# A fused attention and MLP kernel: batch 2 transposed by the DMA crossbar, and an order of steps written out as a list

## The chip, the cores and the metric

The kernel runs on one core of a Trainium2 chip. The metric is the device time in microseconds of one execution. Engines are named as the profile names them: PE is TensorE (matmuls), with PEld its weight loads, DVE is VectorE, ACT is ScalarE, POOL is GpSimd, and SP is SyncE, which here only issues DMAs.

## The reference

There are 8 batches of 8 heads, 576 rows each, head size 64, and 32 "packed" queries p for each head. Attention is done twice: p attends to k and v, and then q attends to that packed result as both keys and values. Its output (4608 rows of 512) goes through an MLP with a hidden width of 2048 and a squared relu.

```python
def sm_attn(qq, kk, vv):
    s = scale * np.matmul(qq, kk.transpose(0, 1, 3, 2))
    ...
    a = a / (np.sum(a, axis=-1, keepdims=True) + 1e-09)
    return np.matmul(a, vv)
p_packed = sm_attn(p, k, v)
out = sm_attn(q, p_packed, p_packed)
...
r = np.maximum(x @ w_in, 0.0)
return (s * (r * r) + b) @ w_out
```

## The kernel before, in words

All inputs are float32 in memory. The loads go through POOL's DMA queue, which turns them into bfloat16 on the way. Each of k, q and v of a batch is one tile of 96 x 3072 from a pool of five buffers (the tag "raw"), which reordered copies of q and v share.

A batch goes through these steps. Each is a small function whose instructions are issued in the order in which the functions are called:

- `prep_p` transposes p on TensorE into `pbd`. `twice_p` first doubles p in its own tile with a VectorE copy.
- `prep_k(b, half)` transposes half of the keys with 12 TensorE transposes and one VectorE copy; `prep_q(b, half)` does the same for half of the queries with 24 transposes, a ScalarE copy and a VectorE copy. For later batches `dma_k` and `dma_q` do these transposes with the DMA crossbar from SP's queue instead; `dma_q` needs a reordered copy of q, made by `order_q` with two VectorE copies. `order_v` reorders v in the same way for a denser form of the matmuls in `packed`. Which form `packed` takes is set by the constant `N_PE_T`: batches below it are transposed on TensorE.
- `first_scores(b, qd)`: scores of p against k for half of the heads, and their exp on ScalarE. `packed(b, qd)`: weights times v, and the sums of the weights; with the second half VectorE makes `ppc` and the reciprocals `rd` and `rs`.
- `second_scores(b)`: q against the packed result, and the exp. `weights(b, qd)`: column sums by a matmul, logarithm and exp of their negative on ScalarE, and a VectorE product, which gives `aT`.
- `packed_w` (two quarters of w_in at a time) or `packed_w1` (one quarter): the packed result times w_in, scaled into `pw` by ScalarE and VectorE. The attention output itself is never formed: `mlp_in(b, m)` multiplies `pw` with `aT` for one of 16 blocks of the hidden width, ScalarE takes the relu into `rlu`, VectorE squares it into `gT`.
- `Out.step(n)`: n of the 16 matmuls of `gT` with `w_out` for one group of 128 output rows. With the last, VectorE applies s and the bias row `biasrep` into `ysb`, and SP stores it. The bias row itself is 16 matmuls (`bias_part`).

PSUM has three double banks for all steps but the last (tile `hps`), and two single banks for the outputs (tile `yps`). A step that needs a double bank waits until an earlier one has been read out.

The order is pinned for each engine: TensorE, VectorE, ScalarE, POOL and SP each work through their instructions as the code calls them. Up to batch 2's scores the calls are written out one below the other, with `idle(n)` in between: n dummy matmuls on a tile of zeros, 42 in all. Batches 0 and 1 share one MLP stretch. From batch 2 on, a loop over the 16 blocks m of batch b's MLP places the attention steps of batch b + 1 at fixed blocks, and fills up with output matmuls of the batch before:

```python
        for m in range(NFF):
            mlp_in(b, m)
            for f in steps.get(m, []):
                f()
            fill(per)
```

Of the kernel before, what the change touches and what calls it, by code (L numbers as in the profile page):

```python
# [8 lines left out]
BF16 = mybir.dt.bfloat16  # L9
AF = mybir.ActivationFunctionType  # L10
ALU = mybir.AluOpType


@with_exitstack
def kernel(
# [25 lines left out]
    P = 128  # L41
# [11 lines left out]
    HS = S // 2  # L53
    NT = S // P
    TAIL = S - NT * P
    N_PE_T = 3

    constp = ctx.enter_context(tc.tile_pool(name="constp", bufs=1))
    wpool = ctx.enter_context(tc.tile_pool(name="wpool", bufs=1))
# [36 lines left out]
    def load(store, src, b, tag, h0=0, h1=H):  # L96
        if h0 == 0:
            store[b] = raw(tag).rearrange("r (h x) -> r h x", h=H)
        pool.dma_start(
            out=store[b][:, h0:h1, :],  # L100
            in_=src[b, h0:h1].rearrange("h (r c) d -> r h (c d)", c=NC),
        )

    w_in_sb = wpool.tile([P, NKC, DFF], BF16, name="w_in_sb")
    w_out_sb = wpool.tile([P, NFF, NB], BF16, name="w_out_sb")
    gT = wpool.tile([P, NFF, 3 * S], BF16, name="gT")
# [2 lines left out]
    def load_p(b0, b1):  # L109
        pool.dma_start(  # L110
            out=pn[:, b0:b1, :, 0, :],
            in_=p[b0:b1].rearrange("b (q g) j d -> (g j) b q d", g=4),
        )

    def load_w_in(ch):
        w = moe_w_in[:, ch * NB:(ch + 1) * NB].rearrange("(x k d) f -> x d k f", x=2, d=D)
        for h2 in range(2):
            pool.dma_start(out=w_in_sb[D * h2:D * h2 + D, :, ch * NB:(ch + 1) * NB], in_=w[h2])

    def load_w_out(m0, m1):  # L120
# [7 lines left out]
    vec.memset(identb[:], 0.0)  # L128
    zeros = constp.tile([P, NB], BF16, name="zeros")
    vec.memset(zeros[:], 0.0)  # L130
    load(kn, k, 0, "kn", 0, 4)
    load_p(0, 2)
    load(kn, k, 0, "kn", 4, 8)
    pool.affine_select(
        out=identb[:], in_=identb[:], compare_op=ALU.not_equal, fill=1.0, base=0,
        pattern=[[-1, P]], channel_multiplier=1,
    )
    load(qn, q, 0, "qn")
    load(vn, v, 0, "vn")
    svec = constp.tile([P, 1], F32, name="svec")  # L140
    sp.dma_start(out=svec[:], in_=moe_s[0:1].unsqueeze(0).to_broadcast([P, 1]))
    bvec = constp.tile([P, 1], F32, name="bvec")
    sp.dma_start(out=bvec[:], in_=moe_b[0:1].unsqueeze(0).to_broadcast([P, 1]))
    nc.scalar.preload_act_table_set("natural_log_exp_and_others")
    load(kn, k, 1, "kn")
    load(qn, q, 1, "qn")
    load_w_in(0)
    load(vn, v, 1, "vn")
    load_w_out(0, 4)
    for ch in range(1, NCH):  # L150
        load_w_in(ch)
        load_w_out(4 * ch, 4 * ch + 4)

    KW = H * HS + 32
    kT = [constp.tile([P, KW], BF16, name=f"kT{i}") for i in range(2)]
    qT = [constp.tile([P, NC, HP, R], BF16, name=f"qT{i}") for i in range(2)]
# [16 lines left out]
    def idle(n):  # L173

        t = big()
        for x in range(n):
            mm(t[:, 0, :], zeros[:, 0:P], zeros[:], start=True, stop=True)

    load_p(2, B)


    aT, pw, vr, qr, e1, e2, rd, rs = {}, {}, {}, {}, {}, {}, {}, {}
# [234 lines left out]
    def slot(b):  # L417
        return 1 if b % 2 else (b % 4)
# [5 lines left out]
    def mlp_in(b, m, on_act=True):  # L424
        hps = big()
        for qd in range(NQ):
            for hf in range(2):
                mm(
                    hps[:, hf, 0:HS],
                    pw[b][:, qd, m * P:(m + 1) * P],  # L430
                    aT[b][:, qd, hf * HS:(hf + 1) * HS],
                    start=(qd == 0),
                    stop=(qd == NQ - 1),
                )
        rlu = ysp.tile([P, 2, HS], BF16, tag="rlu", name="rlu")
        if on_act:
            act.activation(out=rlu[:], in_=hps[:, :, 0:HS], func=AF.Relu)
        else:
            vec.tensor_scalar_max(out=rlu[:], in0=hps[:, :, 0:HS], scalar1=0.0)
        g0 = slot(b) * S  # L440
        (vec if on_act else pool).tensor_tensor(
            out=gT[:, m, g0:g0 + S].rearrange("p (a s) -> p a s", a=2),
            in0=rlu[:], in1=rlu[:], op=ALU.mult,
        )

    def bias_part(cps, m):
        mm(cps, onesb[:], w_out_sb[:, m, :], start=(m == 0), stop=(m == NFF - 1))
        if m == NFF - 1:
            vec.tensor_scalar_mul(out=biasrep[:], in0=cps, scalar1=bvec[:])

    def store(ysb, i0, b, col, n):

# [9 lines left out]
    class Out:  # L462


        def __init__(self, col, parts):
            self.col, self.parts, self.m = col, parts, 0

        def step(self, n):

            if self.m == 0:  # L470
                self.yps = psy.tile([P, NB], F32, tag="y", name="yps")
            m1 = min(self.m + n, NFF)
            for m in range(self.m, m1):
                mm(
                    self.yps[:],
                    gT[:, m, self.col:self.col + P],
                    w_out_sb[:, m, :],
                    start=(m == 0),
                    stop=(m == NFF - 1),
                )  # L480
            took = m1 - self.m
            self.m = m1
            if m1 == NFF:
                ysb = ysp.tile([P, NB], F32, tag="ysb", name="ysb")
                vec.scalar_tensor_tensor(
                    out=ysb[:], in0=self.yps[:], scalar=svec[:], in1=biasrep[:],
                    op0=ALU.mult, op1=ALU.add,
                )
                i0 = 0
                for b, col, n in self.parts:  # L490
                    store(ysb, i0, b, col, n)
                    i0 += n
            return took
# [22 lines left out]
        load(qn, q, b, "qn")  # L516
        load(vn, v, b, "vn")

    def m1(b, *ms):
        for m in ms:  # L520
            mlp_in(b, m)

    idle(11)
    twice_p(0, 2)
    prep_k(0, 0)
    prep_p(0)
    idle(7)
    prep_k(0, 1)
    first_scores(0, 0)
    idle(3)  # L530
    first_scores(0, 1)
    prep_p(1)
    idle(3)
    prep_q(0, 0)
    prep_q(0, 1)
    idle(6)
    packed(0, 0)
    packed(0, 1)
    idle(5)
    second_scores(0)  # L540
    prep_k(1, 0)
    prep_k(1, 1)
    weights(0, 0)
    first_scores(1, 0)
    weights(0, 1)
    first_scores(1, 1)
    loads(2)
    idle(3)
    packed_w1(0, 0)
    prep_q(1, 0)  # L550
    prep_q(1, 1)
    m1(0, 0, 1)
    idle(2)
    packed(1, 0)
    packed(1, 1)
    m1(0, 2, 3)
    second_scores(1)
    packed_w1(1, 0)
    idle(2)
    todo = outs(0)  # L560
    t0, t1 = todo[0], todo[1]
    todo = todo[2:]

    def fill(n):
        run_outs(todo, n)

    weights(1, 0)
    t0.step(4)
    weights(1, 1)
    t1.step(4)  # L570
    packed_w1(0, 1)
    m1(1, 0)
    packed_w1(1, 1)
    m1(1, 1, 2, 3)
    for c in range(1, NCH):
        for j in range(4):
            m1(0, 4 * c + j)
            if c > 1 or j > 1:
                (t0 if j % 2 else t1).step(2)
            m1(1, 4 * c + j)  # L580
            if c + 1 < NCH and j > 1:
                packed_w1(j - 2, c + 1)
    twice_p(2, B)
    bps = big()
    for m in range(NFF // 2):
        bias_part(bps[:, 0, :], m)
    prep_p(2)
    prep_k(2, 0)
    for m in range(NFF // 2, NFF):
        bias_part(bps[:, 0, :], m)  # L590
    prep_k(2, 1)
    t0.step(4)
    first_scores(2, 0)
    t1.step(4)
    first_scores(2, 1)
    fill(4)
    loads(3)
    prep_q(2, 0)
    fill(2)
    prep_q(2, 1)  # L600
    fill(4)
    packed(2, 0)
    fill(4)
    packed(2, 1)
    fill(6)
    second_scores(2)
    packed_w(2, 0)
    fill(6)
    weights(2, 0)
    fill(4)  # L610
    weights(2, 1)
    fill(4)
    packed_w(2, 1)
    dma_k(3)
    todo += outs(1)
    fill(10)

    for b in range(2, B):
        a = b + 1
        c = a + 1  # L620
        steps = {}

        def at(m, *fs):
            steps.setdefault(m, []).extend(fs)

        d = 3 if b == 2 else 0
        if b == 2:
            at(1, lambda: (order_q(3), dma_q(3)))
            at(2, lambda: (prep_p(3), order_v(3)))
        if a < B:  # L630
            at(0 + d, lambda: first_scores(a, 0))
            at(1 + d, lambda: first_scores(a, 1))
            at(3 + d, lambda: packed(a, 0))
            at(4 + d, lambda: packed(a, 1))
            at(6 + d, lambda: second_scores(a))
            at(8 + d, lambda: packed_w(a, 0))
            at(9 + d, lambda: weights(a, 0))
            at(10 + d, lambda: weights(a, 1))
            at(12 + d, lambda: packed_w(a, 1))
        if c < B:  # L640
            at(1 + d, lambda: loads(c))
            at(8 + d, lambda: dma_k(c))
            at(10 + d, lambda: (order_q(c), dma_q(c)))
            at(12 + d, lambda: order_v(c))
            at(14, lambda: prep_p(c))
        if b > 2:
            todo = outs(b - 1)
        per = len(todo)
        for m in range(NFF):
            mlp_in(b, m)  # L650
            for f in steps.get(m, []):
                f()
            fill(per)
        fill(NFF * (NT + 1))
    todo = outs(B - 1)
    while todo:
        fill(NFF)
# [1 line left out]
_INS = ['q', 'k', 'v', 'p', 'moe_w_in', 'moe_w_out', 'moe_s', 'moe_b']  # L659
_OUTS = [((4608, 512), 'float32')]  # L660
# [25 lines left out]
```

## Time and profile before

| | |
|---|---|
| median of 7 runs | 269.53 us (268.67 to 271.43) |
| profiled execution | 268.99 us, its span 267.2 us |
| TensorE busy | 249.4 us (93%), 2346 matmuls |
| ScalarE, VectorE busy | 144.2 us (54%), 142.9 us (53%) |
| matmuls into yps | 576, 143.7 us busy |
| matmuls pw x aT | 512, 82.1 us busy |
| dummy matmuls on zeros | 42, 13.7 us busy |
| relu on ScalarE | 128, 650 ns each |
| DMA moved | 34.32 MB, mean 128 GB/s |
| transposes by DMA | 5 of keys (median 5.0 us to landing), 5 of queries (10.4 us) |

Busy time counts an instruction from its start to its end. Matmuls overlap each other, so their busy times add up to more than the time from one start to the next, and a TensorE that is 93% busy still has gaps that the timeline shows better. A bracket at the end of a timeline row gives the idle time of the engine ahead of the row, and what ended it. "PEclk" is the clock that TensorE was granted, as a share of full speed. Time before the first matmul on data, at 7.54 us, is the wait for the first load. All bytes and rates of loads in this document are counted as bfloat16, as they arrive.

### The profile page before, as it was taken

Reading aid. Unit: us, or ns where it says so; the run is one execution under the profiler, and the core shown is the slowest. Engines: PE = TensorE matmul, PEld = TensorE weight load, DVE = VectorE, ACT = ScalarE, POOL = GpSimd, SP = SyncE. Lnnn points to the kernel's source line nnn. Section 1 sums busy time; section 2 is a strip of 40 time slices with the busy share of each in tenths; the row PEclk is TensorE's granted clock in tenths of the full one; section 3 lists DMA queues with packets and bytes.
Section 4 is the critical chain, followed back from the end, with each engine's and each line's share of the span. In section 5 each row is a group of like instructions: output and inputs, shape, how many; then the busy total and the mean of one; then the engine's idle time right before and its main releaser. Section 6 shows DMA issues by size and latency. Waiting matters only on the chain.

```text
span 267.2 us, 5645 instructions
## 1 busy us (share of the span) xinstructions
PE 249.4 (93%) x2346; PEld 139.2 (52%) x2346; DVE 142.9 (53%) x295; ACT 144.2 (54%) x219; POOL 29.4 (11%) x44
## 2 busy tenths in 40 slices
PE   6698889999999999799999999999999999999993
PEld 2364635555535564465556555665565555555441
DVE  2224657676337645765793459456944574444221
ACT  1047689882455537756855575548653773443000
POOL 8243342001000300101030012000000000000000
PEclk9799999999999999999999999999999999999999
DMA  3999999990914999599999969994731113111332
GB/s 39 196 205 204 206 206 196 204 194 4 162 49 94 157 219 177 105 173 198 168 114 154 210 128 161 117 225 92 131 88 42 39 39 82 40 39 42 79 79 79
DMA packets 54634, 34.32 MB, mean 128 GB/s; under 512 B 27472, under 2 KB 50000, under 8 KB 54608
## 3 DMA queue, kind: packets, MB, share of 16 engines
q0 software_dynamic: 25200, 18.61, 48.2%
q1 hardware_dynamic: 29408, 15.34, 26.8%
q8 instruction: 18, 0.29, 0.4%
q14 instruction: 8, 0.07, 0.1%
HBM read 37.23 MB, written 9.44 MB: 175 GB/s over the span
## 4 chain that ended last, share of the span: by engine, by line
PE 71%; DMA 11%; ACT 8%; DVE 6%; issue 2%; POOL 0%; DVEq 0%; ACTq 0%; POOLq 0%
PE yps L71 39%; PE hps L71 30%; DMA qT<-qr 6%; DMA pn<-in_p_dram 3%; PE hps L74 2%; ACT rlu L82 2%; DMA kT<-kn 2%; DVE pw L82 2%; ACT rcd L82 2%; ACT pw L82 2%; ACT e L82 2%; ACT ld L82 1%; DVE qr L82 1%; DVE gT L82 1%; DVE ysb L82 1%
## 5 line engine op out<-in xcount | busy, mean ns | idle before, releaser
L71 PE MATMUL yps<-w_out_sb,gT 128*128 128x512 bf16 x576 | 143.7, 379 | 0.2 <-DVE gT L82 0.2
L82 ACT ACTIVATE rlu<-hps 128x576 bf16<-128x576 f32 x128 | 81.7, 650 | 70.4 <-PE hps L71 63.5
L82 DVE TENSOR_TENSOR gT<-rlu 128x576 bf16<-128x576 bf16 x128 | 58.2, 456 | 67.0 <-ACT rlu L82 65.6
L71 PE MATMUL hps<-aT,pw 128*128 128x288 bf16 x512 | 82.1, 286 | 4.1 <-DVE pbd L82 1.5
L71 PEld LDWEIGHTS <-gT 128*128 128x128 bf16 x576 | 52.9, 98 | 50.3 <-issue 5.7
L71 PEld LDWEIGHTS <-pw 128*128 128x128 bf16 x512 | 49.1, 98 | 38.5 <-issue 5.5
L82 DVE SCALAR_TENSOR_TENSOR ysb<-yps,svec,biasrep 128x512 f32<-128x512 f32 x36 | 26.9, 746 | 14.0 <-PE yps L71 13.8
L82 DVE TENSOR_SCALAR pw<-hps,rd 128x1024 bf16<-128x1024 f32 (+1 forms) x20 | 21.3, 1066 | 4.6 <-ACT pw L82 2.0
L82 ACT ACTIVATE e<-hps 96x768 bf16<-96x768 f32 x16 | 12.8, 799 | 17.7 <-PE hps L71 17.7
L82 ACT ACTIVATE pw<-hps,rd 128x1024 bf16<-128x1024 f32 (+1 forms) x20 | 18.8, 939 | 0.8 <-PE hps L71 0.7
L82 DVE TENSOR_TENSOR aT<-e,rcd 128x576 bf16<-128x576 bf16 x16 | 12.1, 758 | 11.5 <-ACT rcd L82 11.4
L71 PE MATMUL hps<-zeros 128*128 128x512 bf16 x42 | 13.7, 467 | 2.5 <-DVE zeros L82 1.3
L82 POOL DMA_DIRECT2D kn<-in_k_dram x9 | 6.9, 770 | 77.9 <-DMA kT<-kn 52.6
L82 ACT ACTIVATE e<-hps,rs 128x576 bf16<-128x576 f32 x16 | 10.9, 738 | 8.0 <-PE hps L71 8.0
L71 PE MATMUL hps<-w_in_sb,ppc 64*32 64x512 bf16 x256 | 11.5, 382 | 1.1 <-ACT e L82 0.7
L82 ACT ACTIVATE rcd<-ld 128x576 f32<-128x576 f32 x16 | 10.9, 683 | 0.5
L82 ACT ACTIVATE ld<-hps 128x576 f32<-128x576 f32 x16 | 10.3, 643 | 1.0 <-PE hps L71 1.0
L82 POOL DMA_DIRECT2D vn<-in_v_dram x8 | 6.2, 774 | 42.2 <-PE hps L74 28.0
L71 PE MATMUL hps<-pbd,kT 128*128 128x64 bf16 x192 | 8.7, 193 | 1.5 <-DVE kT L82 0.9
L71 PEld LDWEIGHTS <-kT 128*128 128x128 bf16 x192 | 7.9, 98 | 3.4 <-DVE kT L82 1.3
L71 PEld LDWEIGHTS <-ppc 64*32 64x32 bf16 x384 | 4.2, 89 | 9.7 <-issue 8.6
L71 PEld LDWEIGHTS <-zeros 128*128 128x128 bf16 x42 | 4.5, 117 | 7.9 <-issue 5.4
(45 smaller groups left out, 114.9 us busy)
## 6 DMA issues: line engine op xcount, KB each, us to landing
qn<-in_q_dram POOLq DMA_DIRECT2D x8, 576.0 KB, 13.3
vn<-in_v_dram POOLq DMA_DIRECT2D x8, 576.0 KB, 13.5
out_dram<-ysb SPq DMA_DIRECT2D x24, 192.0 KB, 2.3
kn<-in_k_dram POOLq DMA_DIRECT2D x7, 576.0 KB, 9.4
out_dram<-ysb SPq DMA_DIRECT2D x24, 128.0 KB, 2.8
w_in_sb<-in_moe_w_in_dram POOLq DMA_DIRECT2D x8, 256.0 KB, 15.1
w_out_sb<-in_moe_w_out_dram POOLq DMA_DIRECT2D x4, 512.0 KB, 15.5
out_dram<-ysb SPq DMA_DIRECT2D x24, 64.0 KB, 2.0
```

The lines of the kernel that those rows point to most:

```text
L71: return tc.keep_in_program_order(nc.tensor.matmul(*a, **kw))
L74: return tc.keep_in_program_order(nc.tensor.transpose(*a, **kw))
L82: return lambda *a, **kw: tc.keep_in_program_order(f(*a, **kw))
```

## The change

Four things change.

1. Batch 2 takes the crossbar's way: its `prep_k` and `prep_q` become `dma_k` and `order_q` with `dma_q`, and `packed` takes the reordered v (`N_PE_T` goes from 3 to 2).
2. Batch 0's q is loaded in two halves, each in two DMAs (`load_pairs`), and its p alone; batch 1's p follows alone, and the rest later.
3. Everything up to the end of batch 2's MLP, and batch 3's attention in it, is called from a list of words, `ORDER`, which was worked out offline on a simulator. All dummy matmuls but one (the word z) are gone. MLP blocks and output steps stand in the list one by one and out of sequence; the bias matmuls come in eight pairs.
4. From batch 3 on the loop is as before.

The form of `mlp_in` without ScalarE also changes, but no word of the list uses it.

```diff
-    N_PE_T = 3
+    N_PE_T = 2
...
+    def load_pairs(store, src, b, tag, half):
+
+        if half == 0:
+            store[b] = raw(tag).rearrange("r (h x) -> r h x", h=H)
+        for h2 in range(2):
+            h0 = HP * h2 + 2 * half
+            pool.dma_start(
+                out=store[b][:, h0:h0 + 2, :],
+                in_=src[b, h0:h0 + 2].rearrange("h (r c) d -> r h (c d)", c=NC),
+            )
...
-    idle(11)
-    twice_p(0, 2)
-    prep_k(0, 0)
-    prep_p(0)
-    idle(7)
...
+    words = {
+        "k": lambda b: load(kn, k, b, "kn"),
...
+        "kh": lambda b, x: load(kn, k, b, "kn", 4 * x, 4 * x + 4),
+        "qh": lambda b, x: load_pairs(qn, q, b, "qn", x),
...
+        "p": lambda b0, b1: load_p(b0, min(b1, B)),
+        "win": load_w_in,
+        "wout": lambda ch: load_w_out(4 * ch, 4 * ch + 4),
+        "mask": mask,
+        "z": lambda: idle(1),
+        "pp2": lambda b0, b1: twice_p(b0, min(b1, B)),
+        "pT": prep_p,
+        "kT": prep_k,
+        "qT": prep_q,
+        "kD": dma_k,
+        "qo": order_q,
+        "qD": dma_q,
+        "vo": order_v,
+        "s": first_scores,
+        "a": packed,
+        "c": second_scores,
+        "w": weights,
+        "e": packed_w1,
+        "E": packed_w,
+        "m": lambda b, m: mlp_in(b, m),
...
+        "t": lambda t: y[t].step(2),
+        "b": bias_step,
+    }
+    for word in ORDER.split():
+        name, *args = word.split(".")
+        words[name](*(int(x) for x in args))
```

The list of words, in which kD.2 is `dma_k(2)` and m.0.5 is `mlp_in(0, 5)`:

```
kh.0.0 mask qh.0.0 z p.0.1 kh.0.1 v.0 pp2.0.1 qh.0.1 k.1 win.0 p.1.2 q.1 kT.0.0 win.1 qT.0.0 pT.0
v.1 wout.0 win.2 win.3 kT.0.1 s.0.0 wout.1 s.0.1 wout.2 a.0.0 qT.0.1 a.0.1 pp2.1.2 v.2 c.0 w.0.0
kT.1.0 e.0.0 w.0.1 pT.1 kT.1.1 q.2 m.0.0 m.0.2 s.1.0 m.0.1 s.1.1 qT.1.0 m.0.3 qT.1.1 a.1.0 a.1.1
e.0.1 c.1 wout.3 t.0 w.1.0 k.2 t.1 m.0.4 t.0 e.1.0 w.1.1 m.0.6 m.0.5 m.0.7 p.2.8 m.1.3 e.1.1 t.1
e.0.2 m.1.0 t.1 t.0 m.1.2 m.0.8 m.0.9 t.1 e.0.3 m.1.4 t.1 e.1.2 t.0 m.1.5 m.0.10 t.0 m.1.6 m.0.12
m.0.11 m.0.13 kD.2 m.0.14 m.1.8 t.1 qo.2 m.0.15 m.1.9 vo.2 b.0 pp2.2.8 k.3 e.1.3 b.1 m.1.11 b.2 v.3
b.3 b.4 t.1 t.0 t.0 b.5 pT.2 b.6 b.7 m.1.7 t.1 t.0 m.1.14 m.1.1 qD.2 m.1.13 m.1.10 t.2 s.2.0 q.3 t.3
t.3 s.2.1 t.2 t.3 t.3 a.2.0 t.2 pT.3 t.3 kD.3 a.2.1 m.1.12 t.3 q.4 t.2 E.2.0 t.3 t.3 m.1.15 t.2 c.2
t.2 t.2 t.2 t.4 t.4 t.4 w.2.0 t.5 t.4 w.2.1 E.2.1 t.5 qo.3 t.5 t.4 v.4 t.5 t.4 qD.3 t.4 t.5 pT.4 t.5
t.4 m.2.2 s.3.0 m.2.10 t.6 t.6 vo.3 m.2.7 s.3.1 m.2.15 t.5 t.6 a.3.0 m.2.12 m.2.0 t.6 a.3.1 m.2.3
t.5 m.2.6 t.6 m.2.13 t.6 t.6 t.6 m.2.4 m.2.1 t.7 k.4 m.2.14 c.3 t.7 vo.4 t.8 t.7 E.3.0 m.2.8 kD.4
t.7 t.8 t.7 w.3.0 m.2.9 t.8 t.8 w.3.1 t.8 m.2.5 t.7 t.7 E.3.1 t.7 t.8 t.8 m.2.11 qo.4 qD.4 t.8
```

More of the change, by code (lines that the diff above doesn't have):

```diff
@@ L11 @@
 ALU = mybir.AluOpType
+ORDER = """
+kh.0.0 mask qh.0.0 z p.0.1 kh.0.1 v.0 pp2.0.1 qh.0.1 k.1 win.0 p.1.2 q.1 kT.0.0 win.1 qT.0.0 pT.0
[10 more added lines that the diff above has]
+t.7 t.8 t.7 w.3.0 m.2.9 t.8 t.8 w.3.1 t.8 m.2.5 t.7 t.7 E.3.1 t.7 t.8 t.8 m.2.11 qo.4 qD.4 t.8
+"""
 @with_exitstack
@@ L130 @@
     vec.memset(zeros[:], 0.0)
[L131 to L139, printed above, removed]
     svec = constp.tile([P, 1], F32, name="svec")
@@ L144 @@
     nc.scalar.preload_act_table_set("natural_log_exp_and_others")
[L145 to L152, printed above, removed]
     KW = H * HS + 32
@@ L177, in idle @@
             mm(t[:, 0, :], zeros[:, 0:P], zeros[:], start=True, stop=True)
-    load_p(2, B)
     aT, pw, vr, qr, e1, e2, rd, rs = {}, {}, {}, {}, {}, {}, {}, {}
@@ L434, in mlp_in, with bias_part @@
                 )
-        rlu = ysp.tile([P, 2, HS], BF16, tag="rlu", name="rlu")
+        g0 = slot(b) * S
+        dst = gT[:, m, g0:g0 + S].rearrange("p (a s) -> p a s", a=2)
         if on_act:
+            rlu = ysp.tile([P, 2, HS], BF16, tag="rlu", name="rlu")
             act.activation(out=rlu[:], in_=hps[:, :, 0:HS], func=AF.Relu)
+            vec.tensor_tensor(out=dst, in0=rlu[:], in1=rlu[:], op=ALU.mult)
         else:
[L439 to L449, printed above, removed]
+            vec.scalar_tensor_tensor(
+                out=dst, in0=hps[:, :, 0:HS], scalar=0.0, in1=hps[:, :, 0:HS],
+                op0=ALU.max, op1=ALU.mult,
+            )
+    def bias_part(bps, m0, m1):
+        for m in range(m0, m1):
+            mm(bps, onesb[:], w_out_sb[:, m, :], start=(m == 0), stop=(m == NFF - 1))
+        if m1 == NFF:
+            vec.tensor_scalar_mul(out=biasrep[:], in0=bps, scalar1=bvec[:])
     def store(ysb, i0, b, col, n):
@@ L465, in __init__ @@
         def __init__(self, col, parts):
-            self.col, self.parts, self.m = col, parts, 0
+            self.col, self.parts, self.m, self.yps = col, parts, 0, None
         def step(self, n):
-            if self.m == 0:
+            if self.yps is None:
                 self.yps = psy.tile([P, NB], F32, tag="y", name="yps")
@@ L517, in loads @@
         load(vn, v, b, "vn")
-    def m1(b, *ms):
-        for m in ms:
-            mlp_in(b, m)
-    idle(11)
-    twice_p(0, 2)
-    prep_k(0, 0)
-    prep_p(0)
-    idle(7)
[L528 to L618, printed above, removed]
+    y = outs(0) + outs(1) + outs(2)
+    bias = {}
+    def bias_step(x):
+        if x == 0:
+            bias["ps"] = big()[:, 0, :]
+        bias_part(bias["ps"], 2 * x, 2 * x + 2)
@@ new lines, in mask @@
+    def mask():
+        pool.affine_select(
+            out=identb[:], in_=identb[:], compare_op=ALU.not_equal, fill=1.0, base=0,
+            pattern=[[-1, P]], channel_multiplier=1,
+        )
+    words = {
+        "k": lambda b: load(kn, k, b, "kn"),
+        "q": lambda b: load(qn, q, b, "qn"),
+        "v": lambda b: load(vn, v, b, "vn"),
+        "kh": lambda b, x: load(kn, k, b, "kn", 4 * x, 4 * x + 4),
+        "qh": lambda b, x: load_pairs(qn, q, b, "qn", x),
+        "vh": lambda b, x: load_pairs(vn, v, b, "vn", x),
+        "p": lambda b0, b1: load_p(b0, min(b1, B)),
[18 more added lines that the diff above has]
+        "m": lambda b, m: mlp_in(b, m),
+        "n": lambda b, m: mlp_in(b, m, False),
+        "t": lambda t: y[t].step(2),
+        "b": bias_step,
+    }
@@ L619 @@
+    for word in ORDER.split():
+        name, *args = word.split(".")
+        words[name](*(int(x) for x in args))
+    for b in range(3, B):
         a = b + 1
@@ L624, in at @@
             steps.setdefault(m, []).extend(fs)
[L626 to L629, printed above, removed]
         if a < B:
[L631 to L639, printed above, removed]
+            at(0, lambda: first_scores(a, 0))
+            at(1, lambda: first_scores(a, 1))
+            at(3, lambda: packed(a, 0))
+            at(4, lambda: packed(a, 1))
+            at(6, lambda: second_scores(a))
+            at(8, lambda: packed_w(a, 0))
+            at(9, lambda: weights(a, 0))
+            at(10, lambda: weights(a, 1))
+            at(12, lambda: packed_w(a, 1))
         if c < B:
[L641 to L644, printed above, removed]
+            at(1, lambda: loads(c))
+            at(8, lambda: dma_k(c))
+            at(10, lambda: (order_q(c), dma_q(c)))
+            at(12, lambda: order_v(c))
             at(14, lambda: prep_p(c))
-        if b > 2:
-            todo = outs(b - 1)
+        todo = y[9:] if b == 3 else outs(b - 1)
         per = len(todo)
@@ L652 @@
                 f()
-            fill(per)
-        fill(NFF * (NT + 1))
+            run_outs(todo, per)
+        run_outs(todo, NFF * (NT + 1))
     todo = outs(B - 1)
     while todo:
-        fill(NFF)
+        run_outs(todo, NFF)
 _INS = ['q', 'k', 'v', 'p', 'moe_w_in', 'moe_w_out', 'moe_s', 'moe_b']
```

## The prediction

> **What bounds the kernel now.** I read the windows first (busy time, clock and DMA by stretch), then the timeline for the gaps of each engine, then the queues.
>
> ```profile
> core 0: us, PE busy (x) PEld busy (x) DVE busy (x) ACT busy (x) POOL busy (x), PEclk, DMA share, GB/s
> 7.50:20.00 12.50, 10.78 (x181) 6.68 (x182) 3.75 (x10) 2.79 (x4) 3.92 (x7) 0.86 1.31 203
> 20.00:33.00 13.00, 10.88 (x219) 7.29 (x225) 6.51 (x16) 8.92 (x15) 4.26 (x8) 1.00 1.26 205
> 33.00:61.00 28.00, 25.33 (x217) 14.38 (x217) 18.91 (x37) 24.08 (x41) 4.87 (x6) 1.00 1.29 195
> 66.00:113.00 47.00, 43.71 (x481) 23.61 (x479) 26.32 (x53) 26.45 (x38) 3.78 (x5) 1.00 0.73 135
> 113.00:263.00 150.00, 149.28 (x1206) 82.85 (x1205) 81.98 (x161) 80.02 (x120) 6.24 (x9) 1.00 0.63 111
> ```
>
> From 113 to 263 us TensorE never rests, and the change leaves that part as it is. Up to 61 us the loads run at a constant 195 to 205 GB/s: the time at which a tile lands there is bytes in front of it divided by 0.205 MB/us. TensorE's 10.8 busy us before 20 and 20 to 33 hold 6.3 and 2.4 us of dummy matmuls (the same windows on the tile "zeros"), so the opening waits for data. The gaps from 33 to 113 are the prize. The largest, by the timeline:
>
> ```profile
> 38.76 0.40 PE L71 MATMUL hps<-aT,pw 128*128 128x288 bf16 x2 [0.84 <-DVE aT L82]
> 76.31 0.62 PE L71 MATMUL hps<-w_in_sb,ppc 64*32 64x512 bf16 x15 [0.66 <-ACT e L82]
> 88.79 0.51 PE L71 MATMUL hps<-pbd,kT 128*128 128x64 bf16 x12 [0.54 <-DMA kT<-kn]
> 112.98 0.65 PE L71 MATMUL hps<-aT,pw 128*128 128x288 bf16 x4 [1.48 <-DVE pbd L82]
> ```
>
> The bracket is idle time and what ended it. The last row opens batch 3's loop: that loop begins at 112.98.
>
> **TensorE's work, step by step.** Times are from one start to the next where nothing waits: m (4 matmuls of 288) 0.49 us (112.98 to 113.47), t (2 of 512) 0.43 (84 in 18.14), s 0.35, a 0.65 in batches 0 and 1 and 0.51 in the vr form (94.19 to 94.70), c 0.37, w 0.25, e 0.34, E 0.56, half a key transpose 0.51, half a query transpose 0.64, pT 0.11, the bias 3.45. The word list has 48 m, 72 t, 8 s, 8 a, 4 c, 8 w, 8 e, 4 E, 4 kT, 4 qT, 5 pT: 79 us. Before needs 2.6 us more: for batch 2 two key halves (1.0), two query halves (1.3) and 2 x 0.14 in packed. Of those 79 us, 12.8 stand ahead of the first t and 66.4 from it on.
> From second_scores(1), at 32.61, to 112.98 the kernel before takes 80.4 us, and its work in these units is 66.4 + 2.6 + 0.4 (c) + 0.3 (an e that comes earlier now) = 69.7. So 10.7 us are gaps and two dummies: all that a new order can win there, besides the 2.6.
>
> **Loads: the opening wins nothing.** A POOL DMA issues about 0.8 us apart, and eight may be under way:
>
> ```profile
> 13.15 0.78 POOL L82 DMA_DIRECT2D vn<-in_v_dram  x1 [4.75 <-PE hps L74]
> 16.66 0.61 POOL L82 DMA_DIRECT2D w_in_sb<-in_moe_w_in_dram  x1 [1.34 <-DMA vn<-in_v_dram]
> 22.41 0.61 POOL L82 DMA_DIRECT2D w_in_sb<-in_moe_w_in_dram  x1 [2.10 <-DMA qn<-in_q_dram]
> 27.82 0.61 POOL L82 DMA_DIRECT2D w_in_sb<-in_moe_w_in_dram  x1 [2.22 <-DMA vn<-in_v_dram]
> ```
>
> The releases date landings: v0 16.66, q1 22.41, v1 27.82. The new queue puts w_in chunk 1 (0.52 MB, 2.6 us) ahead of v1, so v1 lands at 30.4; the split q and p add three issues (2.4 us of POOL, hidden by the queued bytes after 8 us). By the same division: v0 15.3, second half of q0 16.7, k1 19.6, w_in 0 22.2, q1 25.2, w_in 1 27.7, w_out 0 33.2, w_out 1 40.9, q2 49.2, w_out 3 51.8, k2 54.6, p of batches 2 to 7 55.6, k3 58.5. Batch 0 gets through some 2 us earlier, then packed(1,0) waits for v1: at 30.6, then 1.3 us of packed and 0.9 us to scaled results, c at about 32.5, the first t when w_out 0 lands, 33.2. That is where the kernel before stands too (32.61).
>
> **From 33.2 on.** 33.2 + 66.4 = 99.6 without any wait. I add:
> - ScalarE and w_out 1: between c.1 and the ninth t it has two exps (1.37), two weights (2.7), five relu (0.56 each, six in a row took 3.37) and two e (1.36), 8.2 us beside 5.6 of TensorE; and t.1's third step needs w_out 1 at 40.9 where the sum stands at 39.3. Together 2.0.
> - From there to batch 2's scores 21 relu and 4 e are 14.6 of some 20 us: 0.8 of small waits.
> - p for batch 2: VectorE waits at twice_p from about 53 to 55.6, with e.1.3's halves and squares of m behind it; prep_p(2) comes at 57.3. Nothing, while p lands before that; 1 us for each us later.
> - Batch 2's transposes on SP. Its prices:
>
> ```profile
> 83.61 3.13 SPq L82 DMA_TRANSPOSE kT<-kn  x1
> 111.54 2.88 SPq L82 DMA_TRANSPOSE qT<-qr  x1
> 134.18 7.81 SPq L82 DMA_TRANSPOSE qT<-qr  x1
> 104.04 1.11 SPq L82 DMA_DIRECT2D out_dram<-ysb  x2
> ```
>
> The first landed after 5.05 us with idle DMA; over five, kT lands in 4.8 to 6.5 and qT in 4.9 to 16.7 (median 10.4; the third row took 16.73, with loads issued beside it). kD.2 starts when k2 lands, 54.6, with k3 and v3 in flight: 61 if it shares with them, 71.3 at the longest; its scores stand at 62. I take 0.5. qD.2 stands behind four stores of t.1 and t.0 (0.56 us each, ready at 60): issued at 62.2, landing 67 to 79; the median for a disturbed one less the lighter load gives 71.5, where c.2 stands at 70.5. I take 1.0. Two pairs of reorder copies (0.51 us a copy, 2.0) replace two key copies (1.5), two query copies on VectorE (0.9) and two on ScalarE (1.3): nothing.
> - Small waits in batches 2 and 3: 1.0 (the old stretch 66 to 113 had over 4, mostly the end where no t was left; now t.8 stands up to the last word).
> - qD.4 now comes with the last words, 10.4 us before its use at batch 4's second_scores, where it had 12.3; and the clock (below): 0.6 together.
> Sum 5.9: batch 3's loop begins at 105.5 instead of 113.0, 7.5 us earlier, and the rest keeps its length:
>
> ```profile
> 244.72 18.14 PE yps L71 x84
> 262.89 0.75 DVE ysb L82
> ```
>
> The profiled execution took 268.99 us (span 267.2 and 1.8 around it): 261.5. It is 0.54 below the median 269.53, so for the median 262.0.
>
> **A rule against the change: the clock.** The dummies go (42, one stays). Before, one-us windows give PEclk 1.00 at 7 to 8, then 0.75, 0.50, 0.50, 0.54, and 1.00 after 12, although TensorE's gap had been only 1.9 us; dummies took 0.43 us each there, against 0.22 later. The Trainium skill ("TensorE: Matmul & The Clock Gate", Part 1 and "Why this matters for your kernels") asks for no gap over about 3 us, and in Part 4 says that transposes do not count as busy. By the row alone, the clock is half whenever the last 2 us were thin, to about 23 us, where work is dense: 6.4 us of work become 12.8, inside the waits for v0, k1 and w_in 0. By the rule the opening, mostly transposes, stays cold until the first m, and the 3 us wait for v1 could cool it again: 3.4 us at half speed after 30.6, 1.7 us lost, of which ScalarE's and w_out's 2.0 hide most. So 0 by the row, 0 to 1.7 by the rule; I took the row's end, 0.3, in the term above.
>
> **Rivals.**
> - The order meets almost no waits: batch 3's loop at 100.0 (99.6 and 0.4), 13.0 us earlier than 113.0, so 256.5. For it: t steps stand between nearly all links. Against: ScalarE's 8.2 beside 5.6. Chance 0.12.
> - ScalarE becomes the bound to 62 us: 26 relu at the isolated 0.65, six e, two weights and exps are 25 us of 26; at the 86% that it reached from 33 to 61 that is 29, 3 more than TensorE's: 265.5. Chance 0.12.
> - Slower: the crossbar under load. The Trainium skill ("DMA: Bandwidth & Descriptors", "Issuing engines are not separate DMA queues") has all queues on one set of engines; the 16.73 us row shows what that costs, the 5.05 row what it costs alone. If kD.2 takes 16.7, scores wait 9.3 us at 62; if qD.2 then runs through only after it, another 16.7 to 88 where c.2 would stand at 80: 17.5 in place of 1.5, 278. It decides against the change once the two cost over 9 us together. For it: k3 and v3 are queued at just that time, and the old kernel had these transposes on a busy TensorE for 2.3 us in all. Against: a transpose's own DMA work is one load's, some 3 us. Chance, with the like, 0.21.
> - It does not do what it says: the order is pinned for each engine in both kernels, so it is followed; only a wait at the one place that sets the end could leave the time, 269.5. Chance 0.05.
> - As summed, 258 to 266: 0.50.
>
> A measurement of this kernel tells 0.5% (1.35 us) from no change. Faster by more 0.73, within 0.06, slower 0.21. The range for 8 in 10 goes from 255.5 (start at 99, all hidden) to 273 (half of the crossbar's price).
>
> **What would show it.** Right: packed(1,0) near 30.6; batch 3's first m near 105; ScalarE over 90% busy from 33 to 41; from 113 on nothing changed but the shift. Each step: a TensorE gap ended by w_out near 41; one ended by kT or qT near 62 and 71, under 2 us each; none ended by pbd near 57. Wrong: v1 landing before 29; PEclk at 0.5 after 33; a gap over 4 us ended by a transpose; first_scores(4,0) or second_scores(4) waiting for DMA.

## The result, and the profile after

In 27 executions the changed kernel took 262.79 to 278.03 us, median 271.08; the kernel before, in 64 executions beside them, 268.65 to 271.66, median 269.51. The comparison of the two keeps only executions within 1.5% of a kernel's own fastest, so that a ratio, here and in the experiments, can differ from that of the medians; of the changed kernel these are five, 262.79 to 265.50: their ratio to the kernel before is 0.979 (95% interval 0.9756 to 0.9823), 263.9 us. Both numbers are true of this kernel. Its five quickest executions gain 5.7 us of the 7.5 that were forecast, and 17 of the 27 gain nothing. The scatter goes with TensorE's clock: the five had a mean granted clock of 0.990 to 0.993, those over 271 us one of 0.967 to 0.981.

The profiled execution is one of the long ones, 271.35 us with a span of 269.6. The gaps over 0.7 us of TensorE's timeline between 28 and 165 us, which were those at 38.76 and 112.98 before, are now two others:

```profile
76.30 0.68 PE L87 MATMUL hps<-qT,ppc 64*32 64x288 bf16 x16 [5.58 <-DMA qT<-qr]
114.53 0.52 PE L87 MATMUL hps<-pbd,kT 128*128 128x64 bf16 x12 [3.26 <-DMA kT<-kn]
```

The first row is c.2 (`second_scores(2)`), which waits for qD.2; the second is `first_scores(4, 0)`, which waits for kD.4. On the page, the granted clock in 40 slices of 6.7 us falls after each of them:

```profile
PEclk9999999999959999979999999999999999999999
```

The windows show it finer (busy time and instructions of PE, PEld, DVE, ACT and POOL, then granted clock, DMA share and GB/s):

```profile
64.00:70.00 6.00, 6.00 (x79) 3.33 (x77) 3.03 (x8) 2.25 (x3) 0.78 (x1) 1.00 1.42 98
70.00:72.00 2.00, 0.71 (x5) 0.20 (x2) 1.32 (x3) 0.65 (x1) 0.00 (x0) 1.00 1.38 159
72.00:74.00 2.00, 0.00 (x0) 0.00 (x0) 0.00 (x0) 0.00 (x0) 0.00 (x0) 1.00 1.33 173
74.00:76.00 2.00, 0.00 (x0) 0.00 (x0) 0.00 (x0) 0.00 (x0) 0.00 (x0) 0.57 1.30 187
76.00:78.00 2.00, 1.71 (x19) 0.59 (x20) 0.00 (x0) 0.96 (x2) 0.00 (x0) 0.50 1.28 192
78.00:80.00 2.00, 2.00 (x6) 0.73 (x5) 0.31 (x1) 0.41 (x1) 0.00 (x0) 0.50 1.26 182
80.00:82.00 2.00, 2.00 (x9) 0.82 (x8) 0.44 (x1) 0.00 (x0) 0.00 (x0) 0.73 1.70 120
82.00:84.00 2.00, 2.00 (x24) 0.74 (x23) 0.60 (x1) 1.94 (x4) 0.00 (x0) 1.00 1.00 87
```

All five engines stand still from 72 to 76 while the DMA columns stay full. TensorE then looks fully busy from 78 to 82, at half its clock up to 80 and 0.73 of it up to 82. What the DMA engines carry is in the timelines of SP and POOL:

```profile
54.16 5.67 SPq L98 DMA_TRANSPOSE kT<-kn  x1
62.30 3.36 SPq L98 DMA_TRANSPOSE qT<-qr  x1
65.78 12.94 SPq L98 DMA_TRANSPOSE kT<-kn  x1
...
62.44 0.77 POOL L98 DMA_DIRECT2D vn<-in_v_dram  x1 [8.72 <-DMA kT<-kn]
63.20 0.77 POOL L98 DMA_DIRECT2D qn<-in_q_dram  x1
67.73 0.78 POOL L98 DMA_DIRECT2D qn<-in_q_dram  x1 [3.76 <-PE hps L87]
```

When kD.2 lands, at 61.9, it frees a raw buffer. POOL was waiting for just that (8.72 us), and it issues v of batch 3 in the same moment in which SP issues qD.2; q of batches 3 and 4 follow, and on SP kD.3. qD.2 lands at 76.25, 13.95 us after its issue.

### The profile page after: what moved, and what is told of

It reads as the page before. It is cut to its first block, busy times and chain, and to the rows that moved or that the text cites. A ratio compares the mean times of both kernels' runs of the same rounds, so it can differ in the third digit from the quotient of the medians.

```text
span 269.6 us, 5379 instructions
## 1 busy us (share of the span) xinstructions
PE 243.7 (90%) x2209; PEld 138.4 (51%) x2209; DVE 142.4 (53%) x297; ACT 142.7 (53%) x217; POOL 32.3 (12%) x48
## 3 DMA queue, kind: packets, MB, share of 16 engines
q1 hardware_dynamic: 34080, 16.52, 33.2%
## 4 chain that ended last, share of the span: by engine, by line
PE 73%; DMA 14%; ACT 6%; DVE 4%; issue 1%; POOL 1%; POOLq 0%; DVEq 0%
PE yps L87 40%; PE hps L87 30%; DMA kT<-kn 6%; DMA qT<-qr 5%; DMA qn<-in_q_dram 2%; PE hps L90 2%; ACT e L98 2%; ACT rlu L98 1%; ACT rcd L98 1%; ACT ld L98 1%; DVE pw L98 1%; DVE ysb L98 1%; DVE qr L98 1%; ACT qT L98 1%; DVE gT L98 1%
## 5 line engine op out<-in xcount | busy, mean ns | idle before, releaser
L87 PE MATMUL yps<-w_out_sb,gT 128*128 128x512 bf16 x576 | 146.6, 385 | 0.0
L98 ACT ACTIVATE rlu<-hps 128x576 bf16<-128x576 f32 x128 | 81.3, 650 | 71.7 <-PE hps L87 66.4
L87 PEld LDWEIGHTS <-gT 128*128 128x128 bf16 x576 | 53.7, 99 | 53.0 <-issue 10.3
L87 PEld LDWEIGHTS <-pw 128*128 128x128 bf16 x512 | 49.8, 99 | 33.1 <-issue 2.5
L98 POOL DMA_DIRECT2D qn<-in_q_dram x11 | 8.0, 738 | 20.3 <-DMA kT<-kn 11.8
L90 PE MATMUL hps<-identb,kn 96*128 96x96 bf16 x48 | 4.6, 280 | 5.8 <-DMA kn<-in_k_dram 5.8
```

Source lines behind the costliest of these rows:

```text
L87: return tc.keep_in_program_order(nc.tensor.matmul(*a, **kw))
L90: return tc.keep_in_program_order(nc.tensor.transpose(*a, **kw))
L98: return lambda *a, **kw: tc.keep_in_program_order(f(*a, **kw))
```

## The experiments

Two theories stood against each other. *Contention*: qD.2 is late because loads that nobody needs yet share the DMA engines with it. *The crossbar itself*: a transpose in this place is slow because of the transposes around it, and batch 2 is better left on TensorE.

**The changed kernel once more** (c0_changed_again), no edit, to see the scatter in another set of executions.

> The changed kernel as it is, to stand on the same chip beside the others. Theory A (crossbar under load): its time varies by several us from run to run, 262 to 275, because batch 2's query transpose (issued at 62.3, landed at 76.25 in the profile) sometimes comes in time and sometimes stops TensorE for over 3 us, after which its clock is halved for a few us. Theory B (the variation is the chip's and not the kernel's): all variants of this set scatter alike.

Twelve executions: 267.00 to 277.82 us, median 272.51; ratio 0.997 (0.9911 to 1.0028). None came near 263. The same two gaps, 5.90 and 2.87 us, stood in its profile. So two profiles of two show them, and short executions are the exception: 5 of 39.

**Batch 2 back on TensorE, in the new order** (e1_batch2_on_tensore).

```diff
-    N_PE_T = 2
+    N_PE_T = 3
...
-m.0.13 kD.2 m.0.14 ... qo.2 m.0.15 m.1.9 vo.2 ... m.1.1 qD.2 m.1.13 ... a.2.0 t.2 pT.3 t.3 kD.3
+m.0.13 m.0.14 ... m.0.15 m.1.9 ... m.1.1 kT.2.0 kT.2.1 m.1.13 ... a.2.0 qT.2.0 t.2 pT.3 t.3 qT.2.1 kD.3
```

> Batch 2 back on TensorE in the new order: its key transposes stand where qD.2 stood, its query transposes around pT.3; the words kD.2, qo.2, qD.2, vo.2 are gone. TensorE gets 2.6 us more work. Theory A (crossbar under load): the gap at second_scores(2) (5.6 us and about 1.8 us of halved clock) is gone, the time is 263 to 266 and scatters by under 3 us, unless batch 4's late keys (second gap, 3.3 us and 1.7 us of clock) remain; with them up to 269. Theory B (scatter is the chip's): as wide as the changed kernel and 2.6 us slower than it, 265 to 275.

Six executions in two groups: 262.56, 263.93 and 264.08, and 269.52 to 274.43 (ratio 0.9769, 0.9721 to 0.9817). In the profiled execution, one of the long ones (273.56 us), the gap at c.2 is gone, and another stands at `second_scores(4)`:

```profile
123.05 0.68 PE L87 MATMUL hps<-qT,ppc 64*32 64x288 bf16 x16 [6.04 <-DMA qT<-qr]
```

qD.4 was issued at 108.53 beside loads of batch 5 (issued at 104.39 and 108.67). Taking the crossbar away from batch 2 doesn't end the waits, so *the crossbar itself*, as a matter of batch 2, is not enough to explain them.

**qD.2 ahead of kD.2** (e2_qD2_first): SP's order alone.

```diff
-m.0.11 m.0.13 kD.2 m.0.14 m.1.8 t.1 qo.2 m.0.15 ... m.1.1 qD.2 m.1.13
+m.0.11 m.0.13 m.0.14 m.1.8 t.1 qo.2 qD.2 kD.2 m.0.15 ... m.1.1 m.1.13
```

> Only SP's queue changes: batch 2's query transpose is issued right after its reorder copy (about 53 us), ahead of the key transpose, instead of behind the stores of the first two output groups (62.3). Theory A (under load, and late in SP's queue): the query transpose lands by 60, second_scores(2) waits for nothing (5.6 us and 1.8 us of clock less than in the profiled run), and the key transpose lands 1 to 3 us later than 61.9, which its first use shows as a gap of 1 to 4 us. Time 263 to 267. Rival (what delays the transposes is the sum of bytes, not their place): the wait only moves to the keys, 4 us or more there, and the time stays at 268 to 272.

274.99 us (273.09 to 281.43, seven executions), ratio 1.0173 (1.0122 to 1.0223). The wait moved to the keys and doubled:

```profile
73.01 0.82 PE L87 MATMUL hps<-pbd,kT 128*128 128x64 bf16 x12 [11.60 <-DMA kT<-kn]
```

kD.2 was issued at 56.68 and landed at 73.0, with loads of batch 3 issued at 53.10 and 54.99. The query transpose, now first, took 13.5 us to landing beside the same loads. In this profile, too, a second wait stood at `second_scores(4)`, of 6.64 us.

**Batch 4 loaded keys first** (e3_k4_before_q4): k, v, q in place of q, v, k.

```diff
-t.3 q.4 t.2 E.2.0 ... k.4 m.2.14
+t.3 k.4 t.2 E.2.0 ... q.4 m.2.14
```

> Only POOL's queue changes: batch 4 is loaded in the order k, v, q instead of q, v, k. Theory A: k4 is issued at about 68 instead of 97.9, so batch 4's key transpose is no longer held by its load, first_scores(4,0) waits for nothing (3.3 us and 1.7 us of clock less in runs that had the gap), while second_scores(2) still waits: 266 to 270 and still scattered. Rival (the second gap is only the first one passed on, through SP's queue and the buffers): no difference to the changed kernel.

The second gap, at `first_scores(4, 0)`, was gone, the one at c.2 stayed (6.46 us), and a third came up:

```profile
129.42 0.68 PE L87 MATMUL hps<-qT,ppc 64*32 64x288 bf16 x16 [6.41 <-DMA qT<-qr]
```

The time stayed at 271.87 us (267.90 to 277.09, twelve executions; ratio 1.0027, 0.9982 to 1.0073). This third wait is at `second_scores(4)`, as in e1 and e2: with batch 4's keys in time, its queries are the late ones.

**The crossbar alone, in the old order** (e4_crossbar_in_old_order): the kernel before, with only batch 2's transposes changed.

```diff
-    N_PE_T = 3
+    N_PE_T = 2
...
+    dma_k(2)
+    order_q(2)
+    dma_q(2)
+    order_v(2)
     twice_p(2, B)
-    prep_k(2, 0)
...
-    prep_q(2, 1)
```

> The kernel before with one part of the change alone: batch 2 by the crossbar, its SP and VectorE steps put ahead of twice_p(2, B), where the old order leaves the DMA engines idle (61 to 66 us: DMA share 0.00). Theory A (a crossbar transpose costs what else is in the DMA engines): with nothing beside it both transposes land 5 us after their issue, well ahead of their use; TensorE loses 2.6 us of transposes and nothing waits, 266.5 to 268, little scatter. Rival (batch 2's transposes by crossbar are harmful as such): slower than before by 2 us or more.

268.40 us (267.17 to 273.76, twelve executions), ratio 0.9941 (0.9908 to 0.9973), by which it is 1.6 us faster. Batch 3's loop began at 111.21, 1.8 earlier than before, of TensorE's 2.6 us that went. Part of the rest went into a wait for p's doubling, which now stood behind four reorder copies on VectorE:

```profile
64.13 0.28 PE L74 MATMUL hps<-identb,pn 128*128 128x128 bf16 x2 [1.91 <-DVE pn L82]
```

The DMA engines were not idle here, as the expectation had it. The freed buffers let q and v of batch 3 start at once beside qD.2:

```profile
62.69 3.24 SPq L82 DMA_TRANSPOSE qT<-qr  x1
...
62.90 1.01 POOL L82 DMA_DIRECT2D qn<-in_q_dram  x1 [3.43 <-DVE qr L82]
63.91 0.77 POOL L82 DMA_DIRECT2D vn<-in_v_dram  x1
```

qD.2 took 10.0 us to landing in place of 5, and came half a microsecond ahead of c.2, at 73.24. So this kernel has the contention too, and room for it.

**Batch 3's loads held until qD.2 has landed** (e5_loads_held_for_qD2). POOL reads one column of `qT` before it may issue the next load; the rest of the order stays.

```diff
+    held = constp.tile([P, 1], BF16, name="held")
+
+    def hold(b):
+        pool.tensor_copy(out=held[:], in_=qT[b % 2][:, 0, 0, 0:1])
...
-m.1.11 b.2 v.3 ... m.1.1 qD.2 m.1.13
+m.1.11 b.2 ... m.1.1 qD.2 hold.2 v.3 m.1.13
```

> The changed kernel with one copy of a column of qT put into POOL's queue behind batch 2's query transpose, so that the loads v3, q3, q4 and all later ones start only when it has landed; nothing else moves. Theory A (loads beside the transpose hold it up): issued at 62.3, it lands by 68, second_scores(2) (70.7) waits for under 1 us, the TensorE clock stays at 1.00 there; the later keys of batch 4 may still cost up to 5 us: 263 to 268. Rival (the transposes of batch 3's keys, issued right behind on the same queue, are what holds it up): it lands at 72 or later, and the gap stays at 2 us or more.

qD.2 was issued at 63.60, and the small copy that waits for it ran at 70.10:

```profile
70.10 0.19 POOL L98 COPY held<-qT 128x1 bf16<-128x1 bf16 x1 [15.01 <-DMA qT<-qr]
```

6.5 us in place of 13.95, though kD.3 still came right behind it on SP, at 67.05. That is *contention*, and it is with the loads: the next transpose in the queue did no such harm once they were gone. (Which part of the way the loads and the transpose share, no run here separates.) c.2 had no gap. The time moved only to 269.66 us (265.49 to 272.26, twelve executions; ratio 0.9917, 0.9868 to 0.9965), since `second_scores(4)` now waited 4.70 us for its transpose, as in e1, and two smaller waits of 1.95 and 1.62 us stood ahead of it.

**Both held, and keys of batch 4 first** (e6_held_twice_k4_first): e5, with e3's order and a second `hold` behind qD.4, ahead of batch 5's loads.

```diff
-t.7 t.8 t.8 m.2.11 qo.4 qD.4 t.8
+t.7 t.8 t.8 m.2.11 qo.4 qD.4 hold.4 t.8
```

> As the run with loads held for batch 2's query transpose, with batch 4 loaded in the order k, v, q as well, and batch 5's loads held in the same way for batch 4's query transpose. Theory A: both gaps go (first_scores(4,0) and second_scores(4) wait under 1 us each), TensorE keeps its clock, and the time is 261 to 264 with a scatter of under 3 us. Rival: holding loads makes the next ones late, and a gap ended by kT or qT of batch 3 or 5 of over 2 us comes in their place: 265 or more.

261.43 us (260.16 to 264.14, six executions), ratio 0.968 (0.962 to 0.974), span 259.2 at a clock of 1.000. Batch 3's first m stood at 105.32. One gap over a microsecond was left ahead of it, and its cause is a held load, q of batch 3, for whose reorder copy VectorE waits with `pbd` behind it:

```profile
82.82 0.66 PE L87 MATMUL hps<-aT,pw 128*128 128x288 bf16 x4 [1.79 <-DVE pbd L98]
...
81.24 1.02 DVE L98 COPY qr<-qn 96x1536 bf16<-96x1536 bf16 x2 [2.17 <-DMA qn<-in_q_dram]
```

**Batch 2 on TensorE, with qD.4 held** (e7_TensorE_and_held): e1 with `hold.4`, so that it differs from e6 mainly in batch 2's way.

> Batch 2 back on TensorE in the new order, and batch 5's loads held behind batch 4's query transpose. Theory A: the one gap that the TensorE version had in its profile (6.0 us at second_scores(4), ended by qT) goes, and its times gather at the low end, 262 to 265. Rival: the gap comes from something else than batch 5's loads: times between 262 and 274 as without the hold.

262.40 us (261.19 to 266.58, six executions), ratio 0.9714 (0.9658 to 0.977), no gap over 0.6 us after 28. Its interval overlaps that of e6, and the medians lie 1 us apart; but e6 still has its gap of 1.79 us, so the two don't yet show what the crossbar is worth for batch 2 (f4 below does). Without the crossbar, the order and the hold have 7.7 us by the ratio.

**The opening.** Three kernels on top of e6 test what dummies and loads are worth there: f1_dummies_back puts 35 dummy matmuls back where TensorE waits, f2_v1_before_win1 loads v of batch 1 ahead of w_in chunk 1, and f3_dummies_and_v1 does both.

```diff
-kh.0.0 mask qh.0.0 z p.0.1 ... c.0 w.0.0 kT.1.0 e.0.0 w.0.1
+kh.0.0 mask qh.0.0 i.13 p.0.1 ... i.3 c.0 i.4 w.0.0 kT.1.0 e.0.0 i.2 w.0.1
```

```diff
-q.1 kT.0.0 win.1 qT.0.0 pT.0 v.1 wout.0
+q.1 kT.0.0 v.1 qT.0.0 pT.0 win.1 wout.0
```

> The kernel with loads held twice and k4 first, with 35 dummy matmuls back in the opening (13 ahead of the first transpose, the others in the waits to 23 us), so that TensorE's clock is full from 7.5 us. Theory R (the row's end: the cold opening hides in waits for loads, packed(1,0) waits for v1 anyway): the steps before 26 us get shorter, packed(1,0) still starts at 30.2 to 30.5, and the time is the same within 0.5 us. Rival (the rule of the clock: the cold opening costs up to 1.7 us): 1 to 1.7 us faster.

> The same kernel (loads held twice, k4 first), v1 loaded ahead of w_in's chunk 1. v1 then lands at 27.8 instead of 30.3. Theory R: packed(1,0) is freed at 27.8; but the cold TensorE reaches it only at 29.5 to 30.3, so the gain is 0 to 0.8 us, and the step behind it, the first t, waits for w_out's chunk 0 at about 33 as before: same within 0.5 us. Rival (the load is all that holds the opening): 2 us faster.

> Both: dummies in the opening and v1 ahead of w_in's chunk 1. Theory R: packed(1,0) starts at about 28, second_scores(1) 2 us earlier than 32.3, and the first t then waits for w_out's chunk 0 (33): 0 to 1 us faster than either alone. Rival: clock and load each hold the opening, and together they give 2 to 3 us.

With the earlier v of batch 1, `packed(1, 0)` came at 30.67 where e6 had 30.56. It waited for VectorE's copy of the queries both times, so the load alone does not hold this place: 263.07 us (260.81 to 264.88, six executions; ratio 0.9719, 0.9671 to 0.9766). The dummies cost time: 266.89 us (264.32 to 267.46; 0.9866, 0.9818 to 0.9913) and, with the load, 266.22 (265.64 to 266.71; 0.9854, 0.9812 to 0.9895), which by the ratios is 5.0 us more than e6 and 3.6 more than f2. Neither theory had that, and `packed(1, 0)` came late, at 32.17 in f1. There the clock was full until 20, then:

```profile
20.00:24.00 4.00, 2.19 (x13) 0.76 (x14) 2.19 (x4) 2.02 (x4) 1.84 (x3) 0.77 1.33 203
24.00:28.00 4.00, 4.00 (x25) 2.60 (x24) 2.09 (x4) 1.05 (x2) 1.45 (x3) 0.50 1.28 204
```

TensorE waited for w_in here (0.56 and 0.88 us), was busy for 2.19 of 4 us, and went into the dense m of 24 to 28 at half clock. That pace is no loss against e6, where the first eight matmuls of m took the same 2.12 us. What is lost is the time of the dummies themselves, which at half clock stand in front of the work:

```profile
23.85 1.44 PE L87 MATMUL hps<-zeros 128*128 128x512 bf16 x3 [0.74 <-ACT ld L98]
25.08 0.42 PE L90 MATMUL hps<-identb,pn 128*128 128x128 bf16 x2
```

The second row, `prep_p(1)`, is at 23.37 in e6, and the first t came at 34.51 (e6: 32.90). The rest of the 5 us is a shift further on: c.2 waited 1.33 us, and the wait of e6 for q of batch 3 became 4.14 us with half clock behind it. Why these grew is open. What the clock alone costs in the opening, these three don't separate.

**The load that was held too long, first** (f4_q3_before_v3): e6 with q of batch 3 ahead of v.

```diff
-m.1.1 qD.2 hold.2 v.3 m.1.13 m.1.10 t.2 s.2.0 q.3 t.3
+m.1.1 qD.2 hold.2 q.3 v.3 m.1.13 m.1.10 t.2 s.2.0 t.3
```

> The same kernel (loads held twice, k4 first), q3 loaded ahead of v3. In that kernel's profile the reorder copy of q3 waits 2.2 us on VectorE for the load (81.2), and TensorE 1.8 us at 82.8 for prep_p(4)'s copy queued behind it. Theory A: q3 lands some 3 us earlier, both waits go, 1.5 to 2 us faster: 259 to 260.5. Rival: v3, now later, holds its own reorder copy and the gap comes back at packed(3,0): same time.

258.70 us (258.25 to 259.53, six executions), ratio 0.9583 (0.9546 to 0.962): it beats both kernels, with the scatter down to 1.3 us from the changed kernel's 15. Batch 3's first m stands at 103.19, and no gap over 0.73 us is left after 40. The stretch in which the changed kernel stood still:

```profile
62.80 3.65 SPq L98 DMA_TRANSPOSE qT<-qr  x1
...
68.15 0.19 POOL L98 COPY held<-qT 128x1 bf16<-128x1 bf16 x1 [13.99 <-DMA qT<-qr]
...
71.15 0.44 PE L87 MATMUL hps<-qT,ppc 64*32 64x288 bf16 x16
...
72.00:74.00 2.00, 2.00 (x11) 0.94 (x10) 0.78 (x2) 1.03 (x2) 0.00 (x0) 1.00 1.19 153
74.00:76.00 2.00, 2.00 (x26) 0.83 (x24) 0.03 (x1) 1.40 (x3) 0.77 (x1) 1.00 1.15 169
```

The copy that waits for qD.2 runs 5.35 us after its issue, 3 us before c.2 asks for it. POOL's bracket of 13.99 us costs nothing, since no load that POOL holds back is needed in that time.

Against e7, f4 also shows what the crossbar does for batch 2. The first m of batch 3's loop, in e7 and then in f4:

```profile
105.45 0.65 PE L87 MATMUL hps<-aT,pw 128*128 128x288 bf16 x4
...
103.19 0.65 PE L87 MATMUL hps<-aT,pw 128*128 128x288 bf16 x4
```

f4 is 2.3 us earlier, of the 2.6 us of transposes that TensorE no longer does, and by the ratios 3.5 us faster, with the intervals apart. The two differ in the order of loads as well, but neither has a gap over 0.75 us there, so little but TensorE's own work is left to differ.

## Why the prediction was right or wrong

**Right: where the gain sits, and its size without the two waits.** With both waits removed the loop of batch 3 begins at 105.32 (e6) or 103.19 (f4); the sum had 105.5. Without its terms for qD.2, batch 4 and the clock (1.6) the sum has 4.3 us of waits behind the first t, and f4 has 103.19 - 33.12 - 66.4 = 3.7. From there to the last VectorE instruction f4 takes 149.65 us and the kernel before 149.91. The five short executions, 263.9 us, are 1.9 above the 262.0. That the comparison comes so near is luck in part, since it rests on these five: the median of all 27, 271.08, misses the 262.0 by 9 us. And three of the four signs of being wrong that were named stood in the profiled execution: half clock after 33, a gap over 4 us ended by a transpose, and `first_scores(4, 0)` waiting for a DMA.

**Right: the opening gains nothing.** `packed(1, 0)` came at 30.36 and the first t at 32.69, where the working had 30.6 and 33.2. But the reason given, v of batch 1 landing at 30.4, is only one of two that end within 0.1 us of each other. In e5 that load did end the wait, at 30.32; f2 brought it forward, and TensorE still stood there until 30.67, for the copy of the queries.

**Right in kind, half the size: 2.0 for ScalarE and w_out 1.** From 33 to 41 TensorE was busy for 7.07 of 8 us, ScalarE for 7.94, and the two waits over 0.3 us (0.35 and 0.47) were ended by ScalarE. From 41 to 61 TensorE never rested. The gap ended by w_out near 41, named as a sign, did not appear. kD.2 cost 0.65 us at 61.90 (0.5 in the sum).

**Mis-sized: "I take 1.0" for qD.2.** In the profiled execution c.2 waited 5.58 us. The working knew of 67 to 79 for the landing, and chose 71.5 by the median of the transposes before; it landed at 76.25. The row of 16.73 us, which it showed with loads beside it, was the nearest to this place and went to the slower rival alone. Here kD.2's landing itself releases a load, and a second and a third follow, which are needed much later. This was to be seen in the list of words and the count of raw buffers: five, and POOL queued up for the next one.

**Mis-sized: 0.6 for batch 4's transposes and the clock.** The term looked at qD.4. The late one was kD.4, because batch 4's k is loaded last, so that its transpose is issued at 104.73 and lands at 114.49: 3.26 us at `first_scores(4, 0)`.

```profile
97.89 0.77 POOL L98 DMA_DIRECT2D kn<-in_k_dram  x1 [9.98 <-DMA out_dram<-ysb]
...
104.73 6.18 SPq L98 DMA_TRANSPOSE kT<-kn  x1
```

In e1, e2, e3 and e5, whose keys of batch 4 were there in time, it was `second_scores(4)` and qD.4 after all.

**The clock: weighed at the wrong place.** It was put at 0 to 1.7 us in the opening and left out behind the waits. In the opening the matmuls ran at half pace until 26.5 us, not only to 23, and behind the wait at 30.36, of 0.32 us, they kept their full pace. Behind the long waits the clock cost more. From c.2 to batch 3's `first_scores(4, 0)`, less that one's own wait, the profiled execution took 34.97 us (114.53 - 3.26 - 76.30); f4 took 32.53. From there to VectorE's last instruction, it took 150.83 and f4 149.16. So half clock cost 2.4 and 1.7 us behind gaps of 5.58 and 3.26. The granted clock gives the same: half of 1.7 and of 2.0 us, and 0.27 of 2.0, are 2.4 in the windows above, and those of 115 to 119 us, at 0.61, 0.50, 0.50 and 0.68, make 1.7.

How long a gap must be is less clear. The Trainium skill ("TensorE: Matmul & The Clock Gate", "Why this matters for your kernels") asks for no gap of more than about 3 us. Here are three gaps, each with a window of one microsecond soon after it, in c0, f3 and f2:

```profile
114.05 0.60 PE L87 MATMUL hps<-pbd,kT 128*128 128x64 bf16 x12 [2.87 <-DMA kT<-kn]
115.00:116.00 1.00, 1.00 (x4) 0.32 (x3) 0.00 (x0) 0.48 (x1) 1.00 (x2) 0.50 1.16 218
...
72.89 0.44 PE L87 MATMUL hps<-qT,ppc 64*32 64x288 bf16 x16 [2.21 <-DMA qT<-qr]
75.00:76.00 1.00, 1.00 (x4) 0.30 (x2) 0.75 (x1) 0.00 (x0) 0.87 (x3) 0.50 0.52 94
...
83.68 0.66 PE L87 MATMUL hps<-aT,pw 128*128 128x288 bf16 x4 [2.68 <-DVE pbd L98]
84.00:85.00 1.00, 0.89 (x6) 0.42 (x5) 0.78 (x2) 0.61 (x1) 0.00 (x0) 1.00 1.31 204
```

The clock fell behind 2.87 and 2.21 us, and it stayed at 1.00 behind 2.68. After 33 us, all gaps of 3.26 us and more halved it, and none of 1.95 or less did. So about 3 us is no safe bound in these runs: between 2.2 and 2.9 both happen. In f1 the clock fell without such a gap.

**The sum of it.** Gaps and clock of the profiled execution are 5.58 + 3.26 + 2.4 + 1.7 = 12.9 us. 271.35 less these is 258.4, and f4, which has neither, took 258.82 in its profiled execution: nothing else of size is open in that one. The prediction had 1.6 for the same four. That the change has its gain and then gives it back is what the slower rival said, with batch 2's two transposes over 9 us as the point of decision. In the profiled execution these two cost 0.65 and 5.58 us and 2.4 of clock, together 8.6; kD.4 added 3.26 and 1.7, and the gain was gone. The rival's picture of one transpose queued through the other was not what happened: e5 and f4 show the loads to be the cause.

**Left open.** None of the executions near 263 us was profiled. That they lack one or both gaps is inferred from their clock of 0.990 to 0.993 and from e1, whose short executions ran at 0.999 and 1.000, its long ones at 0.981 to 0.987. What makes one execution escape is not known.

## What to carry to other kernels

In this order each load was issued as soon as its buffer was free. Such a load can collide with a transpose that is needed next, so let the loads that nobody waits for stand behind the urgent one (one tiny copy on the issuing engine is enough), and among the held ones put that first which is used first. A TensorE gap of over 2 us may cost half clock behind it as well, here another 1.7 to 2.4 us. Look at all executions, not only at the best ones: this kernel scattered over 15 us, and f4, without the two waits, over 1.3.

## What the runs showed of the hardware

- With loads held, qD.2, a crossbar transpose of 96 x 3072, took 5.2 to 6.3 us to landing (f4, e5), even with the next transpose behind it. With two loads beside it it took 10.0 us (e4), and with three and the next transpose 13.9; that next one, kD.3, took 20.6, and SP's issue of it stretched from 2.9 us (e6) to 12.9.
- The clock can fall with no long gap: in f1 no gap from 20 to 24 us was over 0.9 us, but TensorE was busy for only 2.19 of those 4, and the clock went to 0.50.
- The granted clock of the profile is not always TensorE's pace. The kernel after shows 1.00 from 20 to 33, but its matmuls took twice as long until about 26.5:

```profile
24.60 2.06 PE L87 MATMUL hps<-aT,pw 128*128 128x288 bf16 x8
26.85 0.65 PE L87 MATMUL hps<-aT,pw 128*128 128x288 bf16 x4
```

Eight of them take 2.06 us in the first row, where eight at 98.00 us take 1.14; the four of the second row, two microseconds later, are at full pace.
